# Decode by VectorE alone, expert products shared by each stretch's work, and the stacked visits' causal mask added by VectorE

## The chip, the cores and the metric

The kernel runs on one core of one Trainium2 chip. The time is device time in microseconds from one launch; it is given as the median of several runs. The core has TensorE (PE in the profile, its weight loads PEld), VectorE (DVE), ScalarE (ACT), GpSimd (POOL) and SyncE (SP). Each works off its own queue in the order of the program; DMAs are issued from SP's and ACT's queues. Matmul results land in PSUM, everything else lies in SBUF.

## What is computed

Causal attention with a bias, for 8 batches, 8 heads, 576 positions and 64 columns a head, and behind it a feed-forward layer with a maximum over three products, on 4608 tokens of 512 columns (768 hidden). The three up weights and the down weight come as float64.

```
scores = q @ k.T / 8 ;  cum = cumsum(max(s, 0))
scores = where(key > query, -1e9, scores + min(-(cum_q - cum_k), 0))
attn   = softmax(scores) ;  x = attn @ v
out    = max(max(x @ w1, x @ w2), x @ w3) @ w_out
```

## The kernel before

Products are made from two halves of each operand (a high half and the rest), so that three products stand for one in full precision.

**Visits and steps.** A visit is one batch and one pair of heads (tile names: j is the head of the pair). A step is one visit and one block of 128 queries (qb 0 to 3; qb 4 holds the last 64 queries of both heads). The first 8 visits do qb 0 and 1 of batches 0 and 1 (steps 0 to 15), the next 8 do qb 2 to 4 of the same batches (steps 16 to 39), and 24 further visits do all five (steps 40 to 159). These last ones are called stacked: each head's 64 rows of q and k lie above the 64 rows that carry the bias, so a score block takes two products a head, h and l (`scores`, L379), over the first (qb + 1) x 128 keys. Then PE adds the causal mask as one more product a head, a scaled identity times the 128 x 128 tile `tri`, which holds -1e30 above the diagonal (L385).

**A step** t goes like this (L922 to L952). ACT makes prh, the high half of the probabilities, from the exponentials in PSUM and DVE's reciprocal ri. DVE takes the maximum of the next score block, negated, into nm (`highest`, L450), then what stands in the list `middle`, then prl, the low halves (L505). SP transposes prh and prl by DMA into ph and pl. Evictions that are pending follow, then one group of expert products, then the scores of step t + 2 on PE, the exponentials of step t + 1 on ACT (`expo`, L460, bias nm), then the work that the lists put at this step (`todo`), then more expert groups, and last the value products av of a visit whose probabilities were completed the step before (`values`, L574). Scores have two PSUM buffers, so the scores of step t + 2 wait until prh and prl of step t have been read out.

**Expert groups.** A group is 12 products into one PSUM tile pm (L711), or 18 into po for the output (L753). A set of 256 or 320 tokens has 18 pm groups and 4 po groups. A balance `cost[0]` says whether a step takes groups: each step adds an allowance (4200 ns below step 60, then STEP_NS = 4800) less `pe_cost(t)`, an estimate of PE's other work; each group takes off its own time; groups run while the balance is above zero. What is left over after the last step runs as a tail.

**Decode.** Each of the 24 weight tiles r is 128 x 512 doubles, seen as pairs of 32-bit words lo and hi. ACT makes t from hi (`decode1`, L605), POOL multiplies hi by zero so that only its sign remains (`signs`, L609), DVE joins lo's top bits and the sign (`decode2a`, L613) and then t shifted by three (`decode2b`, L620). After a scale is known, ACT rounds a high half into w (`decode3`, L674), and the low half is made by DVE in one instruction (`decode4`, L684), or for every third tile (the set LOW) by POOL in two (L681, L682). `begun`, `split` and `fetched` give the step of each tile's decode, split and load.

A tile is taken from a pool under a tag; a new tile of the same tag waits until the last reader of the old one is done. The transposed probabilities have the tags pTh and pTl with a number: in the first 16 visits it alternates with the visit, later it is the phase (0 for qb 0 and 1, 1 for the others).

Of the kernel before, what the change touches and what calls it, by code (L numbers as in the profile page):

```python
# [21 lines left out]
def kernel(  # L22
# [9 lines left out]
    nc = tc.nc  # L32
# [22 lines left out]
    STEP_NS = 4800.0  # L55
    NSEC = 0.417
    LOW = set(range(2, 24, 3))
# [133 lines left out]
    zero = const.tile([P, 1], F32, name="zero")  # L191
    nc.gpsimd.memset(zero, 0.0)
# [169 lines left out]
    def scores(t):  # L362
# [7 lines left out]
        if stacked(v):  # L370
# [4 lines left out]
            for x in "hl":  # L375
                for j in range(2):
                    w = r[x, j]
                    if qb < 4:
                        nc.tensor.matmul(  # L379
                            ps[:, j, :nk], lhsT=w[:, qs], rhs=w[:, QP:QP + nk], start=(x == "h"), stop=False,  # L380
                            skip_group_check=True,
                        )
            if qb < 4:
                for j in range(2):
                    nc.tensor.matmul(  # L385
                        ps[:, j, qb * P:nk], lhsT=identb, rhs=tri, start=False, stop=True, skip_group_check=True
                    )
                U[t] = (ps[:, :, :nk], nm, nk)
                return
# [57 lines left out]

    def highest(t):
        sc, nm, _ = U[t]
        nc.vector.tensor_reduce(out=nm, in_=sc, axis=AX.X, op=ALU.max, negate=True)  # L450
# [3 lines left out]
    def expo(t):  # L454
        ps, nm, nk = U[t]
        nj = 2 if nk < S else 1
        sm = small.tile([P, 2], F32, tag="sm", name=f"sm{t}")
        for j in range(nj):
            sc = ps[:, j] if nj == 2 else ps
            nc.scalar.activation(  # L460
                out=sc, in_=sc, func=AF.Exp, bias=nm[:, j:j + 1], accum_out=sm[:, j:j + 1]
            )
        se = small.tile([P, 2], F32, tag="se", name=f"se{t}")
        nc.scalar.activation(out=se[:, :nj], in_=sm[:, :nj], func=AF.Copy, scale=1.0 / PSC, bias=EPS / PSC)
        SE[t] = (se, nj)
# [3 lines left out]
    def probs(t):  # L469
# [5 lines left out]
        if qb in (0, 2):  # L475
            PT[v, ph] = [
                att.tile(
                    [P, 4 + 4 * ph, PH[ph][1]], F16, tag=f"pT{c}{v % 2 if v < NP * NB else ph}", name=f"p{c}{t}", bufs=1
                )
                for c in "hl"  # L480
# [47 lines left out]
    RING = [f"w{n}" for n in (10, 11, 12, 13, 14, 15, 16, 17, 22, 23)]  # L528
# [78 lines left out]
    def signs(i):  # L607
        hi = words(i)[1]
        nc.gpsimd.tensor_tensor(out=hi, in0=hi, in1=zero.to_broadcast([P, N]), op=ALU.mult)  # L609

    def decode2a(i):
        lo, hi = (x.bitcast(I32) for x in words(i))
        nc.vector.scalar_tensor_tensor(  # L613
            out=lo, in0=lo, scalar=29, in1=hi, op0=ALU.logical_shift_right, op1=ALU.bitwise_or
        )

    def decode2b(i):
        lo = words(i)[0].bitcast(I32)
        ti = half.pop(i).bitcast(I32)
        nc.vector.scalar_tensor_tensor(  # L620
            out=lo, in0=ti, scalar=3, in1=lo, op0=ALU.logical_shift_left, op1=ALU.bitwise_or
# [54 lines left out]
    def decode4(i):  # L676
        t = words(i)[0]
        w = pairs_w[i // 2][:, i % 2]
        sw = WS["u" if i < 18 else "d"]
        if i in LOW:  # L680
            nc.gpsimd.tensor_tensor(out=t, in0=t, in1=sw.to_broadcast([P, N]), op=ALU.mult)  # L681
            nc.gpsimd.tensor_tensor(out=w[:, 1], in0=t, in1=w[:, 0], op=ALU.subtract)  # L682
        else:
            nc.vector.scalar_tensor_tensor(  # L684
                out=w[:, 1], in0=t, scalar=sw, in1=w[:, 0], op0=ALU.mult, op1=ALU.subtract
            )
# [100 lines left out]
    def pe_cost(t):  # L787
        v, qb = steps[t]
        nk = min((qb + 1) * P, S)
        c = 4 * nk * NSEC + 200.0  # L790
        if qb == 1:
            c += 1152 * 0.417 + 200.0
        if qb == 4:
            c += 3584 * 0.417 + 200.0
        return c
# [31 lines left out]
    fetched = {5: -1, 7: -1, 8: 0, 9: 0, 10: 1, 11: 1, 12: 2, 13: 2, 14: 3, 15: 3, 16: 4, 17: 4}  # L827
    fetched.update({22: 5, 23: 5, 18: 5, 19: 6, 20: 6, 21: 7})
# [13 lines left out]
    parts2 = {}  # L842
    for i, t in sorted(begun.items(), key=lambda x: (x[1], x[0])):
        parts2.setdefault(t + 1, []).append(i)
    for t, ids in parts2.items():
        (amid if t >= 0 else at)(t, decode2a, ids[0])
        for i in ids[1:]:
            at(t, decode2a, i)
        for i in ids:
            at(t, decode2b, i)  # L850
# [165 lines left out]
```

## Time and profile before

| | |
|---|---|
| median of 3 runs | 944.0 us (943.08 to 945.74) |
| profiled execution | 945.22 us |
| its span, first to last instruction | 943.4 us |
| mean granted TensorE clock | 0.962 |
| instructions | 19,983 |
| largest group, the pm products (L711) | 462.9 us, 3456 products |

Busy shares count an engine's own instructions; PE's matmuls overlap each other, so a product's duration is longer than its share of the time. The idle time of a group is put down to the instruction that released it ("<-"). The lines of the profile on which the prediction rests are shown there.

### The profile page before, as it was taken

What the parts mean: (1) busy time and instruction counts of PE and PEld (TensorE: products, weight loads), DVE (VectorE), ACT (ScalarE), POOL (GpSimd) and SP (SyncE); (2) the same over time, 40 slices, a digit from 0 to 9 for tenths busy, and PEclk for the clock granted to TensorE, in tenths of its full rate; (3) what the DMA queues carried; (4) which work ended last, traced back from release to release, by engine and by line L of the source; (5) the groups of instructions that cost most, each with busy time, mean ns of one, the idle gap of its engine ahead of it and who ended that gap; (6) DMA issues with size and microseconds to landing.
All of it is one profiled execution on the core that took longest, in us unless ns stands there. A gap on an engine that the chain in (4) does not pass through costs nothing. (4 is left out here: it accounts for less than half of the span.)

```text
span 943.4 us, 19983 instructions
## 1 busy us (share of the span) xinstructions
PE 838.6 (89%) x7192; PEld 653.2 (69%) x7192; DVE 582.7 (62%) x1184; ACT 569.4 (60%) x1502; POOL 386.8 (41%) x592
## 2 busy tenths in 40 slices
PE   2456768887779899999999998999999999998998
PEld 2444647765556677877887777877887787776876
DVE  6897885666556575667575666576666656563111
ACT  4667566566467576676676676666667666764111
POOL 4455742222433453635453535454455435430211
PEclk9857999999899999999999999999999999999999
DMA  7974236566577678777778677787676676744000
GB/s 277 237 223 88 58 75 140 115 137 150 118 139 144 119 138 162 152 141 136 157 141 155 134 135 135 135 141 145 133 138 148 127 153 102 139 69 96 2 24 28
DMA packets 242035, 122.34 MB, mean 130 GB/s; under 512 B 217808, under 2 KB 226512, under 8 KB 241936
## 3 DMA queue, kind: packets, MB, share of 16 engines
q1 hardware_dynamic: 237904, 108.74, 58.1%
q10 hardware_dynamic: 4032, 12.32, 4.1%
q8 instruction: 57, 0.93, 0.4%
q14 instruction: 42, 0.34, 0.2%
HBM read 60.18 MB, written 9.44 MB: 74 GB/s over the span
## 5 line engine op out<-in xcount | busy, mean ns | idle before, releaser
L711 PE MATMUL pm<-x,w 128*128 128x256 f16 (+1 forms) x3456 | 462.9, 290 | 3.7 <-ACT m L725 1.7
L711 PEld LDWEIGHTS <-w 128*128 128x128 f16 x3456 | 334.2, 99 | 89.6 <-issue 4.1
L505 DVE SCALAR_TENSOR_TENSOR prl<-s,ri,prh 128x512 f16<-128x512 f32 (+3 forms) x288 | 152.8, 567 | 96.6 <-ACT prh L502 50.4
L717 POOL CAST hh<-m 128x256 f16<-128x256 f32 (+1 forms) x96 | 53.5, 557 | 351.4 <-DVE m L728 294.4
L502 ACT ACTIVATE prh<-s,ri 128x512 f16<-128x512 f32 (+3 forms) x288 | 141.8, 538 | 80.8 <-DVE ri L486 71.7
L450 DVE TENSOR_REDUCE nm<-s 128x1 f32<-128x576 f32 (+4 forms) x160 | 128.0, 800 | 49.3 <-PE s L385 28.9
L460 ACT ACTIVATE s<-s,nm 128x512 f32<-128x512 f32 (+4 forms) x288 | 151.2, 525 | 9.2 <-DVE nm L450 4.1
L753 PE MATMUL po<-hh,w 128*128 128x256 f16 (+1 forms) x768 | 150.4, 287 | 1.5 <-DVE w L684 1.5
L728 DVE SCALAR_TENSOR_TENSOR m<-pm,m 128x256 f32<-128x256 f32 (+1 forms) x192 | 87.1, 454 | 97.4 <-PE pm L711 85.0
L753 PEld LDWEIGHTS <-w 128*128 128x128 f16 x1152 | 110.4, 98 | 31.1 <-DVE w L684 2.1
L753 PE MATMUL po<-hl,w 128*128 128x320 f16 (+1 forms) x384 | 110.0, 287 | 0.9 <-POOL hl L718 0.8
L725 ACT ACTIVATE m<-pm 128x256 f32<-128x256 f32 (+1 forms) x96 | 39.1, 407 | 83.9 <-PE pm L711 80.2
L718 POOL TENSOR_TENSOR hl<-m,hh 128x256 f16<-128x256 f32 (+1 forms) x96 | 74.1, 772 | 7.8
L583 ACT ACTIVATE x<-av 128x256 f16<-128x256 f32 (+1 forms) x64 | 26.3, 410 | 78.6 <-PE av L574 77.9
L138 POOL CAST l<-kb 64x576 fp32r<-64x576 f32 x48 | 32.3, 673 | 100.6 <-PE s L394 75.6
L761 ACT ACTIVATE o<-po,os 128x256 f32<-128x256 f32 (+1 forms) x64 | 31.9, 498 | 65.5 <-PE po L753 50.0
L169 POOL TENSOR_TENSOR l<-raw,h 64x576 fp32r<-64x576 f32 x48 | 68.2, 1422 | 7.2 <-ACT h L155 6.0
L584 DVE SCALAR_TENSOR_TENSOR x<-av,x 128x256 f16<-128x256 f32 (+1 forms) x64 | 29.1, 454 | 59.0 <-ACT x L583 58.9
L574 PEld LDWEIGHTS <-vh 128*64 128x64 f16 x832 | 45.0, 112 | 24.6 <-issue 17.1
L574 PE MATMUL av<-pl,vh 128*64 128x320 f16 (+3 forms) x384 | 56.3, 279 | 5.7 <-DMA pl<-prl 5.6
L379 PE MATMUL s<-h 128*128 128x128 f32 (+1 forms) x192 | 53.7, 361 | 8.4 <-DVE prl L505 7.0
L574 PE MATMUL av<-ph,vh 128*64 128x320 f16 (+3 forms) x384 | 57.5, 287 | 0.6 <-DMA ph<-prh 0.6
(142 smaller groups left out, 1148.2 us busy)
## 6 DMA issues: line engine op xcount, KB each, us to landing
raw<-in_qk_dram SPq DMA_DIRECT2D x96, 304.0 KB, 4.7
r<-in_w_dram ACTq DMA_DIRECT2D x20, 512.0 KB, 4.9
rv<-in_qkv_dram SPq DMA_DIRECT2D x32, 320.0 KB, 3.4
out_dram<-o SPq DMA_DIRECT2D x32, 160.0 KB, 2.0
out_dram<-o SPq DMA_DIRECT2D x32, 128.0 KB, 2.3
raw<-in_qkv_dram SPq DMA_DIRECT2D x8, 480.0 KB, 3.9
ph<-prh SPq DMA_TRANSPOSE x192, 3.3
pl<-prl SPq DMA_TRANSPOSE x192, 2.8
```

Of the source, the lines that this page charges most:

```text
L169: nc.gpsimd.tensor_tensor(out=l[far, QP:V0], in0=raw[far, QP:V0], in1=h[far, QP:V0].bitcast(F32), op=ALU.subtract)
L379: nc.tensor.matmul(ps[:, j, :nk], lhsT=w[:, qs], rhs=w[:, QP:QP + nk], start=(x == "h"), stop=False, skip_group_check=True,)
L450: nc.vector.tensor_reduce(out=nm, in_=sc, axis=AX.X, op=ALU.max, negate=True)
L460: nc.scalar.activation(out=sc, in_=sc, func=AF.Exp, bias=nm[:, j:j + 1], accum_out=sm[:, j:j + 1])
L502: nc.scalar.activation(out=hi, in_=src, func=AF.Copy, scale=sc)
L505: nc.vector.scalar_tensor_tensor(out=lo, in0=src, scalar=sc, in1=hi, op0=ALU.mult, op1=ALU.subtract)
L574: nc.tensor.matmul(av[j * D:(j + 1) * D, c0:nq], lhsT=lt, rhs=rt, start=(n < 2), stop=(n >= len(todo) - 2), skip_group_check=True,)
L711: nc.tensor.matmul(pm[:, :nq], lhsT=w[:, wt, kt, :], rhs=xt, start=(n == 0), stop=(n == 3 * NKT - 1))
L717: nc.gpsimd.tensor_copy(out=st["hh"][:, ft, :nq], in_=m1[:, :nq])
L718: nc.gpsimd.tensor_tensor(out=st["hl"][:, ft, :nq], in0=m1[:, :nq], in1=st["hh"][:, ft, :nq], op=ALU.subtract)
L728: nc.vector.scalar_tensor_tensor(out=m1[:, :nq], in0=pm[:, :nq], scalar=HSC, in1=m1[:, :nq], op0=ALU.mult, op1=ALU.max)
L753: nc.tensor.matmul(pm[:, :nq], lhsT=W[18 + ft][:, wt, dt, :], rhs=st[ht][:, ft, :nq], start=(n == 0), stop=(n == 3 * NFT - 1),)
```

## The change

Five things change.

1. **Decode.** POOL's `signs` goes. DVE shifts t by three in place (`shift`), joins lo's top bits into t (`low_bits`), and joins the sign of hi with t into lo (`sign`): three instructions where it had two. All shifts of a step stand ahead of prl, the rest behind. POOL's part of `decode4` goes to DVE.
2. **Masks of stacked visits.** For qb < 4 the two mask products go. DVE runs one fused instruction a head: it adds a slice of a wide bf16 tile `later` (zeros, then `tri`) to the scores, negates, writes the result over the scores and takes the minimum of it. The exponentials use scale -1. `later` is made by POOL at step 20, in the buffer w23, which leaves the ring of x tiles.
3. **Shares.** `pe_cost` now counts what PE runs in the step itself (the scores of step t + 2, the value products that are due), and the allowances are 4400 and 4700 ns. A helper `leave` is added that nothing calls.
4. **Buffers.** The number in pTh and pTl is the phase for every visit.
5. **Loads** of weights are issued up to two steps earlier.

```
-    STEP_NS = 4800.0
+    STEP_NS = 4700.0
-    LOW = set(range(2, 24, 3))
...
-                            ps[:, j, :nk], lhsT=w[:, qs], rhs=w[:, QP:QP + nk], start=(x == "h"), stop=False,
+                            ps[:, j, :nk], lhsT=w[:, qs], rhs=w[:, QP:QP + nk], start=(x == "h"), stop=(x == "l"),
...
-                for j in range(2):
-                    nc.tensor.matmul(
-                        ps[:, j, qb * P:nk], lhsT=identb, rhs=tri, start=False, stop=True, skip_group_check=True
-                    )
...
+    def later_keys():
+        m = wpool.tile([P, Q4], BF16, tag="w23", name="later")
+        nc.gpsimd.memset(m[:, 0:Q4 - P], 0.0)
+        nc.gpsimd.tensor_copy(out=m[:, Q4 - P:Q4], in_=tri)
+        future.append(m)
     def highest(t):
-        sc, nm, _ = U[t]
+        sc, nm, nk = U[t]
+        if below(t):
+            for j in range(2):
+                nc.vector.tensor_tensor_reduce(
+                    out=sc[:, j], in0=sc[:, j], in1=future[0][:, Q4 - nk:Q4], scale=-1.0, scalar=3.0e38,
+                    op0=ALU.add, op1=ALU.min, accum_out=nm[:, j:j + 1],
+                )
+            return
         nc.vector.tensor_reduce(out=nm, in_=sc, axis=AX.X, op=ALU.max, negate=True)
...
-                    [P, 4 + 4 * ph, PH[ph][1]], F16, tag=f"pT{c}{v % 2 if v < NP * NB else ph}", name=f"p{c}{t}", bufs=1
+                att.tile([P, 4 + 4 * ph, PH[ph][1]], F16, tag=f"pT{c}{ph}", name=f"p{c}{t}", bufs=1) for c in "hl"
...
-    def signs(i):
-        hi = words(i)[1]
-        nc.gpsimd.tensor_tensor(out=hi, in0=hi, in1=zero.to_broadcast([P, N]), op=ALU.mult)
+    def shift(i):
+        ti = half[i].bitcast(I32)
+        nc.vector.tensor_scalar(out=ti, in0=ti, scalar1=3, scalar2=None, op0=ALU.logical_shift_left)
+    def low_bits(i):
+        lo, ti = words(i)[0].bitcast(I32), half[i].bitcast(I32)
+        nc.vector.scalar_tensor_tensor(
+            out=ti, in0=lo, scalar=29, in1=ti, op0=ALU.logical_shift_right, op1=ALU.bitwise_or
+        )
+    def sign(i):
+        lo, hi = (x.bitcast(I32) for x in words(i))
         ti = half.pop(i).bitcast(I32)
         nc.vector.scalar_tensor_tensor(
-            out=lo, in0=ti, scalar=3, in1=lo, op0=ALU.logical_shift_left, op1=ALU.bitwise_or
+            out=lo, in0=hi, scalar=-(2 ** 31), in1=ti, op0=ALU.bitwise_and, op1=ALU.bitwise_or
         )
...
     def pe_cost(t):
-        v, qb = steps[t]
-        nk = min((qb + 1) * P, S)
-        c = 4 * nk * NSEC + 200.0
-        if qb == 1:
-            c += 1152 * 0.417 + 200.0
-        if qb == 4:
-            c += 3584 * 0.417 + 200.0
+        c = 0.0
+        if t + 2 < len(steps):
+            nk = min((steps[t + 2][1] + 1) * P, S)
+            c += max(4 * nk * NSEC * 1.09, 480.0) + (100.0 if nk < S else 150.0)
+        for _, ph in due:
+            c += (3584 if ph else 1152) * 0.417 + 200.0
         return c
...
-        cost[0] = min(cost[0] + (4200.0 if t < 60 else STEP_NS) - pe_cost(t), 4000.0)
+        cost[0] = min(cost[0] + (4400.0 if t < 60 else STEP_NS) - pe_cost(t), 4000.0)
```

What this does to the order of the instructions, at three places. First DVE's queue in the fourth step, where two weight tiles are decoded (r the tile's words, t ACT's product of hi, x and av the value products' eviction). Before:

```order
L486 RECIPROCAL ri_446<-se_393 128x2
L450 TENSOR_REDUCE nm_379<-s_378 128x2
L613 SCALAR_TENSOR_TENSOR r_252<-r_252 128x512
L505 SCALAR_TENSOR_TENSOR prl_449<-s_315,ri_446,prh_448 128x2x128 x2
L584 SCALAR_TENSOR_TENSOR x_0_460<-av_0_433,x_0_460 128x256
L639 TENSOR_REDUCE cnu<-gru_395 128x1
L613 SCALAR_TENSOR_TENSOR r_264<-r_264 128x512
L620 SCALAR_TENSOR_TENSOR r_252<-t_425,r_252 128x512
L620 SCALAR_TENSOR_TENSOR r_264<-t_428,r_264 128x512
L330 SCALAR_TENSOR_TENSOR qkl_492<-st_143,qkh_422 128x256
```

The same place of the same queue after the change:

```order
L496 RECIPROCAL ri_450<-se_394 128x2
L462 TENSOR_REDUCE nm_380<-s_379 128x2
L619 TENSOR_SCALAR t_427<-t_427 128x512
L619 TENSOR_SCALAR t_429<-t_429 128x512
L515 SCALAR_TENSOR_TENSOR prl_453<-s_314,ri_450,prh_452 128x2x128 x2
L594 SCALAR_TENSOR_TENSOR x_0_463<-av_0_437,x_0_463 128x256
L649 TENSOR_REDUCE cnu<-gru_396 128x1
L623 SCALAR_TENSOR_TENSOR t_427<-r_248,t_427 128x512
L623 SCALAR_TENSOR_TENSOR t_429<-r_250,t_429 128x512
L630 SCALAR_TENSOR_TENSOR r_248<-r_248,t_427 128x512
L630 SCALAR_TENSOR_TENSOR r_250<-r_250,t_429 128x512
L331 SCALAR_TENSOR_TENSOR qkl_496<-st_141,qkh_424 128x256
```

Two shifts of t now stand ahead of prl where one instruction on r stood, and four instructions follow behind instead of three; nothing on the way reads what POOL writes.

Second, DVE's queue in a stacked visit, at the maxima of its 384 and 512 wide score blocks (m and pm the expert groups' eviction, h part of the next visit's preparation). Before:

```order
L486 RECIPROCAL ri_3844<-se_3784 128x2
L450 TENSOR_REDUCE nm_3774<-s_3773 128x2
L505 SCALAR_TENSOR_TENSOR prl_3847<-s_3722,ri_3844,prh_3846 128x2x128 x2
L584 SCALAR_TENSOR_TENSOR x_1_3857<-av_1_3815,x_1_3857 128x320
L728 SCALAR_TENSOR_TENSOR m_1_0_3855<-pm_1_0_1_3860,m_1_0_3855 128x320
L160 SCALAR_TENSOR_TENSOR h_1_3795<-raw_1_3679,h_1_3795 64x640
L486 RECIPROCAL ri_3906<-se_3884 128x2
L450 TENSOR_REDUCE nm_3874<-s_3873 128x2
L505 SCALAR_TENSOR_TENSOR prl_3909<-s_3773,ri_3906,prh_3908 128x3x128 x2
```

After the change, from the same block on (ISA names the fused instruction, and with nm alone the read of its accumulator):

```order
L496 RECIPROCAL ri_3863<-se_3814 128x2
L457 ISA s_3805,nm_3806<-s_3805,later 128x384
L457 ISA nm_3806 128x1
L457 ISA s_3805,nm_3806<-s_3805,later 128x384
L457 ISA nm_3806 128x1
L515 SCALAR_TENSOR_TENSOR prl_3866<-s_3745,ri_3863,prh_3865 128x2x128 x2
L594 SCALAR_TENSOR_TENSOR x_1_3875<-av_1_3834,x_1_3875 128x320
L163 SCALAR_TENSOR_TENSOR h_1_3827<-raw_1_3688,h_1_3827 64x640
L496 RECIPROCAL ri_3923<-se_3900 128x2
```

Four instructions stand between ri and prl where one stood, and the eviction of an expert group has moved out of this step, since its groups are dealt out otherwise.

Third, SP's queue at the transposes of the first and second visit, with what each waits for (PE is TensorE, Activation ScalarE, DMAHW a transfer). Before:

```order
L508 DMA_TRANSPOSE ph_254<-prh_258 128x2x128 [waits DMAHW6_49,Activation_49]
L508 DMA_TRANSPOSE pl_255<-prl_259 128x2x128 [waits DMAHW7_49,DVE_49]
L508 DMA_TRANSPOSE ph_254<-prh_303 128x4x128 [waits DMAHW2_49,Activation_49]
L508 DMA_TRANSPOSE pl_255<-prl_304 128x4x128 [waits DMAHW3_49,DVE_49]
L508 DMA_TRANSPOSE ph_362<-prh_366 128x2x128 [waits DMAHW6_49,Activation_49]
```

After the change:

```order
L518 DMA_TRANSPOSE ph_252<-prh_256 128x2x128 [waits DMAHW6_49,Activation_49]
L518 DMA_TRANSPOSE pl_253<-prl_257 128x2x128 [waits DMAHW7_49,DVE_49]
L518 DMA_TRANSPOSE ph_252<-prh_303 128x4x128 [waits DMAHW3_49,Activation_49]
L518 DMA_TRANSPOSE pl_253<-prl_304 128x4x128 [waits DMAHW4_49,DVE_49]
L518 DMA_TRANSPOSE ph_364<-prh_368 128x2x128 [waits DMAHW4_49,DMAHW3_49,DMAHW6_49,PE_49,Activation_49]
```

The second visit's first transpose writes the buffer that the first visit's value products read, so it has gained a wait for PE; the rows behind it on SP stand in order.

More of the change, by code (lines that the diff above doesn't have):

```diff
@@ L113, in load_v, with below @@
         R.setdefault(v, {})["rv"] = t.rearrange("p (j k d) -> p j k d", j=2, d=D)
+    def below(t):
+        v, qb = steps[t]
+        return stacked(v) and qb < 4
     def stacked(v):
@@ L526 @@
     done = set()
-    RING = [f"w{n}" for n in (10, 11, 12, 13, 14, 15, 16, 17, 22, 23)]
+    RING = [f"w{n}" for n in (10, 11, 12, 13, 14, 15, 16, 17, 22)]
     def reserve(tag, b, ph):
@@ L678, in decode4 @@
         w = pairs_w[i // 2][:, i % 2]
[L679 to L686, printed above, removed]
+        nc.vector.scalar_tensor_tensor(
+            out=w[:, 1], in0=t, scalar=WS["u" if i < 18 else "d"], in1=w[:, 0], op0=ALU.mult, op1=ALU.subtract
+        )
         fresh[i] = w.rearrange("p h (a c) -> p h a c", c=P)
@@ L787, in pe_cost, with leave @@
     def pe_cost(t):
-        v, qb = steps[t]
-        nk = min((qb + 1) * P, S)
-        c = 4 * nk * NSEC + 200.0
-        if qb == 1:
-            c += 1152 * 0.417 + 200.0
-        if qb == 4:
-            c += 3584 * 0.417 + 200.0
-        return c
+        c = 0.0
[4 more added lines that the diff above has]
+            c += (3584 if ph else 1152) * 0.417 + 200.0
+        return c
+    due = []
+    def leave(t):
+        v, qb = steps[t]
+        return qb in (2, 3, 4) and stacked(v) and visits[v][1] < NP - 1
     todo = {}
@@ L841 @@
         at(first[v] + 1 if v else -2, vscale2, scale_of(v))
-    parts2 = {}
+    together = {}
     for i, t in sorted(begun.items(), key=lambda x: (x[1], x[0])):
[L844 to L850, printed above, removed]
+        together.setdefault(t + 1, []).append(i)
+    for t, ids in together.items():
+        for f in (shift, low_bits, sign):
+            for i in ids:
+                (amid if f is shift and t >= 0 else at)(t, f, i)
     for i, t in split.items():
@@ L896 @@
         at(t, decode3, i)
-    for i, t in sorted(begun.items()):
+    for i, t in begun.items():
         at(t, decode1, i)
-        at(t, signs, i)
-    for n, (i, t) in enumerate(fetched.items()):
-        (amid if t >= 0 and n % 2 == 0 else at)(t, load_w, i, nc.scalar.dma_start)
+    for i, t in fetched.items():
+        at(t, load_w, i, nc.scalar.dma_start)
     at(1, spread, 1)
+    at(20, later_keys)
     prep2(0)
```

20 lines of the change are left out of this document (5 added, 15 removed).

## The prediction

> **What bounds the kernel now.** I read the page's busy shares and slices first, then the table by stretch, the waits, and last the groups of the stretches that differ.
>
> ```profile
> PE 838.6 (89%) x7192; PEld 653.2 (69%) x7192; DVE 582.7 (62%) x1184; ACT 569.4 (60%) x1502; POOL 386.8 (41%) x592
> ...
> PE   2456768887779899999999998999999999998998
> ...
> DVE  6897885666556575667575666576666656563111
> ...
> 14.00:70.00 56.00, 27.82 (x219) 22.06 (x221) 49.59 (x103) 35.61 (x106) 26.76 (x23) 0.76 0.85 230
> 70.00:142.00 72.00, 48.63 (x409) 37.48 (x409) 60.65 (x114) 46.54 (x116) 41.53 (x43) 0.85 0.34 74
> 142.00:268.00 126.00, 104.78 (x892) 79.58 (x893) 75.30 (x141) 74.89 (x185) 34.00 (x50) 0.94 0.63 134
> ...
> 366.00:864.00 498.00, 488.38 (x4324) 387.00 (x4324) 315.20 (x655) 330.89 (x886) 221.24 (x352) 1.00 0.70 135
> ```
>
> The last four rows are stretches: bounds, length, then busy time of PE, PEld, DVE, ACT and POOL, granted clock, DMA share and GB/s. Two kernels stand here. From 366 to 864 us PE is busy 488 of 498 us at full clock; DVE and ACT are at two thirds. There a microsecond of PE work is a microsecond. From 14 to 142 us, where the weights are decoded, PE is busy 76 of 128 us and DVE 110 of 128, with no other engine near it: there DVE's row of work sets the pace. The middle (142 to 268) has no engine that full, and the change does little in it.
>
> **Masks off PE.** The two mask products per stacked step with qb < 4 go: 24 visits x 4 = 96 steps.
>
> ```profile
> 403.31 0.63 PE L379 MATMUL s<-l 128*128 128x512 f32 x2
> 403.78 0.12 PEld L385 LDWEIGHTS <-identb 128*128 128x128 bf16 x2 [0.28 <-issue]
> 403.78 0.28 PE L385 MATMUL s<-tri,identb 128*128 128x128 bf16 x2
> ...
> 403.90 0.27 PE L753 MATMUL po<-hh,w 128*128 128x256 f16 x1
> ```
>
> A matmul's duration overlaps the next one, so the price is from start to start: the pair starts at 403.78, the next product at 403.90, 0.12 us. 96 x 0.12 = **11.5 us**, nearly all of it where PE is full. Bounds: 0, if PE waits instead, and 96 x 0.28 = 27 us, the pair's undivided time.
>
> **The mask on DVE.** Each of these steps replaces one maximum over both heads by two fused instructions (add the mask, write the scores back to PSUM, take the minimum) and two reads of the accumulator.
>
> ```profile
> L450 DVE TENSOR_REDUCE nm<-s 128x2 f32<-128x1024 f32 x20 | 24.3, 1215 | 12.8 <-PE s L385 12.8
> ...
> L450 DVE TENSOR_REDUCE nm<-s 128x2 f32<-128x256 f32 x32 | 13.0, 406 | 2.3 <-PE s L385 2.2
> ...
> L505 DVE SCALAR_TENSOR_TENSOR prl<-s,ri,prh 128x512 f16<-128x512 f32 x96 | 69.1, 748 | 56.8 <-ACT prh L502 26.7 <-ACT tl L502 20.2 <-DMA pl<-prl 8.8
> ...
> L505 DVE SCALAR_TENSOR_TENSOR prl<-s,ri,prh 128x128 f16<-128x128 f32 x64 | 19.4, 344 | 4.2 <-ACT prh L502 3.3 <-DMA pl<-prl 0.2
> ...
> L486 DVE RECIPROCAL ri<-se 128x2 f32<-128x2 f32 x128 | 20.3, 159 | 20.3 <-ACT se L464 19.0
> ...
> L502 ACT ACTIVATE prh<-s,ri 128x512 f16<-128x512 f32 x96 | 62.0, 680 | 32.2 <-DVE ri L486 28.5 <-DMA ph<-prh 3.5
> ```
>
> No row shows the fused instruction, nor a DVE write to PSUM. The nearest is prl: one operand from PSUM, one from SBUF, a write; (748 - 344) / 384 = 1.05 ns an element over a fixed 210 ns. The nearest of a one-column read is 159 ns. A 512-wide step then takes 2 x 748 + 2 x 159 = 1.81 us for 1.22; a 128-wide one 2 x 344 + 2 x 159 = 1.01 for 0.41. So about 0.6 us more of DVE a step, 96 x 0.6 = 58 us. Low end: the extra instructions' fixed parts vanish in the overlap of neighbours and nothing is added. High end: the write to PSUM doubles the time per element, 1280 x 2 elements a visit x 1.05 ns = 2.7 us on top, 24 x 2.7 = 65 us more. At the chosen value DVE's load in the full stretch rises from 63% to some 75%, so it is no bound. Behind the fused pair on DVE stand prl and the evictions of the expert products; for prl's PSUM buffer the scores after next wait. But prl needs ACT's two prh (0.68 us each at 512), which begin together with the maximum, and these cover most of the delay. I take **+2 us**, between 0 and 15.
>
> The Trainium skill (VectorE: DVE Perf Modes, Rules for kernel authors) speaks against this edit: it advises to minimize the number of DVE operations, since each pays its own flush, and four now stand for one. By its cost row for PSUM sources (the TRN2 errata section, 120 cycles and one per element at 0.96 GHz) a 512-wide fused instruction is an estimated 0.66 us, and DVE's part of the sum would be smaller than mine; no run here shows it yet.
>
> **Decode by DVE alone.** POOL loses 24 sign products and 16 instructions of the low halves; DVE gains 24 shifts and 8 low halves.
>
> ```profile
> L613 DVE SCALAR_TENSOR_TENSOR r<-r 128x512 int32<-128x512 int32 x24 | 23.8, 994 | 11.4 <-POOL r L609 11.4
> L620 DVE SCALAR_TENSOR_TENSOR r<-t,r 128x512 int32<-128x512 int32 x24 | 16.9, 734 | 0.1
> L684 DVE SCALAR_TENSOR_TENSOR w<-r,swu,w 128x512 f16<-128x512 f32 x12 | 13.1, 1132 | 0.0
> ...
> L684 DVE SCALAR_TENSOR_TENSOR w<-r,swd,w 128x512 f16<-128x512 f32 x4 | 5.6, 1442 | 0.0
> ...
> 20.52 0.68 DVE L613 SCALAR_TENSOR_TENSOR r<-r 128x512 int32<-128x512 int32 x1
> ...
> 24.44 1.52 DVE L613 SCALAR_TENSOR_TENSOR r<-r 128x512 int32<-128x512 int32 x1 [0.54 <-POOL r L609]
> ...
> 78.09 1.41 DVE L684 SCALAR_TENSOR_TENSOR w<-r,swu,w 128x512 f16<-128x512 f32 x2
> ...
> 91.80 2.61 DVE L684 SCALAR_TENSOR_TENSOR w<-r,swu,w 128x512 f16<-128x512 f32 x2
> ...
> 92.37 1.49 POOL L681 TENSOR_TENSOR r<-r,swu 128x512 f32<-128x512 f32 x1
> ...
> 5.54 0.44 DVE L234 TENSOR_SCALAR r_t<-s_t 64x576 f32<-64x576 f32 x1
> ```
>
> The same DVE instruction takes 0.68 us alone and 1.52 beside a POOL one; a low half 0.70 at 78.09, and 1.30 at 91.80 beside POOL's at 92.37. So the removal frees DVE of the waits for POOL (11.4), of 24 x (0.994 - 0.68) = 7.5, 24 x (0.734 - 0.68) = 1.3, 12 x (1.132 - 0.70) = 5.2 and 4 x (1.442 - 0.70) = 3.0: 28.4 us. Added are 8 x 0.70 = 5.6 and 24 shifts. A shift, with one operand in SBUF, is nearest to L234, 0.44 us at 576 elements, and I take 0.41; as slow as L613 alone it is 0.68. That is 9.8 (16.3) us. Net: DVE's row loses 28.4 - 15.4 = 13 us (6 or 7 at the high price).
>
> The path gains less, for two waits come next. The first is ACT's t, for which all shifts of a step wait ahead of prl:
>
> ```profile
> 74.37 1.51 DVE L613 SCALAR_TENSOR_TENSOR r<-r 128x512 int32<-128x512 int32 x1 [3.36 <-POOL r L609]
> ...
> 73.30 1.04 POOL L609 TENSOR_TENSOR r<-r,zero 128x512 f32<-128x512 f32 x1 [2.56 <-ACT t L605]
> ```
>
> Of DVE's longest wait for POOL, 3.36 us, only the sign's 1.04 goes; the 2.3 before it were for t, behind three w on ACT. The second: the first stretch's transposed probabilities have one buffer where they had two, and the first transposes of a visit wait for the value products of the visit before.
>
> ```profile
> 31.68 1.17 SPq L508 DMA_TRANSPOSE ph<-prh  x1
> ...
> 37.02 0.22 PE L574 MATMUL av<-ph,vl 128*64 128x128 f16 x2
> ...
> 41.74 0.61 ACT L502 ACTIVATE prh<-s,ri 128x128 f16<-128x128 f32 x2
> ...
> ph<-prh SPq DMA_TRANSPOSE x9, 4.6
> ```
>
> The transposes that started at 31.68 would start after the products that end at 37.2, and SP's queue stands behind them. With 4.6 us to land (median of 20 to 70 us) their source is free at 41.8, as prh of two steps later wants it (41.74). The slack is nil, so each of 7 visits may lose what the decode gained there; I put both waits at 3 us together. The path gains **10 us**, between 0 and 17.
>
> **Products shared anew.** The step allowance and the estimate of PE's other work change. In PE's order, of the steps 60 to 159, 15 held a single expert group or none and no value product, now 2; 15 held three or more groups together with the long value product, now none. The tail after the last step has 47 groups for 44, which costs nothing by itself, since the total is fixed. What can go are PE's waits in the thin steps:
>
> ```profile
> PE s L394 <- DVE prl L505: 4.5, 3, 2.2
> PE s L379 <- DVE prl L505: 3.6, 8, 0.9
> ...
> PEld s L379 <- ACT s L460: 12.1, 16, 3.7
> ```
>
> The first two (268 to 864 us) are 8 us of PE itself; weight loads waited 12.1 more, partly ahead of their turn. I take **-6 us**, between +5 (the even steps wait a little everywhere) and -12. The earlier weight loads, the ring with one slot less and the small mask tile on POOL I cost at nothing: POOL is busy 41%, and the loads only move up in ACT's queue.
>
> **Sum.** -11.5 + 2 - 10 - 6 = -25.5 us. The profiled execution took 945.2 us (span 943.4 and 1.8 around it), 1.2 above the median of the runs, 944.0; against the median that is **918.5 us**.
>
> **Rivals.**
> 1. Freed PE time turns into waits: the longer maximum delays prl and with it the scores after next. For it: prl already ends PE's waits above. Against it: DVE idles a third of the time. The masks then give 0 instead of 11.5, and the maximum costs 5: 933.
> 2. The early gain is eaten: ACT's t or the single buffer sets the pace in POOL's place: 918.5 + 10 = 928.5. For it: the nil slack above. Against it: the low halves' part comes after 70 us, when the DMA share has fallen from 0.85 to 0.34 and transposes should land sooner.
> 3. More than forecast: the early stretch gains 17 and the even steps 12: 905.5. The granted clock of 0.76 up to 70 us would rise as PE idles less, and the score products after prl get shorter. The Trainium skill (TensorE: Matmul & The Clock Gate, Part 1) puts half clock to idle windows of about 3.4 us; the 0.76 agrees with gaps of that kind.
> 4. Slower: the fused instruction takes several cycles an element and DVE becomes the bound of the stacked steps. A visit takes 498 / 20 = 24.9 us (20 maxima of 1024 in that stretch) with 315.2 / 20 = 15.8 of DVE, 3.2 of them in the four maxima (by the two rows above). PE needs 24.4 without the masks, so DVE decides when the eight fused instructions and reads take 11.8; less 8 x (0.21 + 0.16) that is 8.8 us for 2560 elements, 3.4 ns each instead of 1.05. At 4.2 ns, four times the row, a visit is 26.3 us: 24 x 1.4 = +34, less 16 from decode and sharing: 962.
>
> That the change does not do what it says is excluded for the masks: their products are gone from PE's order.
>
> **How the numbers follow.** Forecast 0.54 (907 to 930); rival 1 0.14; rival 2 0.13; rival 3 0.12; rival 4 0.07. The range 902 to 938 leaves out rival 4 and the ends of rivals 1 and 3. A measurement of this kernel tells 0.3% from no change, 941 to 947; rival 1 with its maximum at the high price reaches into that. Faster 0.87, same 0.06, slower 0.07.
>
> **What would show it.** Right: DVE in the stacked steps near 75% and PE still at 98%; fused instructions near 0.75 us at 512; the two decode instructions of the new form at 0.68 us with no wait for POOL; PE's waits for prl shorter; and the first 576-wide maximum, now at 133 us, near 123:
>
> ```profile
> 132.96 0.74 DVE L450 TENSOR_REDUCE nm<-s 128x1 f32<-128x576 f32 x1
> ```
>
> Wrong: PE idles more after 300 us, fused rows far over 1 us, or an early stretch as long as before with DVE idle.

## The result and the profile after

The changed kernel takes **918.27 us** (median of 4 runs, 914.14 to 921.02) where the kernel before took 943.54 (4 runs, 940.88 to 945.74): ratio **0.9716**, 95% interval 0.9663 to 0.9769, that is 27 us less (22 to 32). The forecast was 918.5. The profiled execution of the changed kernel is the fastest of its four, 914.14 us, span 912.3 us; differences between the two profiles are therefore some 6 us larger than those between the medians (31.1 us between the profiled executions, 25.3 between the medians).

The page, busy shares and the slices of PE and DVE:

```profile
PE 823.0 (90%) x7000; PEld 645.5 (71%) x7000; DVE 598.3 (66%) x1504; ACT 568.6 (62%) x1502; POOL 345.7 (38%) x553
...
PE   3557769998799989999999999999999999999998
...
DVE  6898886666467766667676767676677657663111
```

The table by stretch, with the same columns as before (bounds, length, PE, PEld, DVE, ACT, POOL, clock, DMA share, GB/s):

```profile
14.00:70.00 56.00, 29.15 (x229) 23.07 (x229) 50.30 (x127) 38.24 (x110) 7.78 (x6) 0.76 0.78 228
70.00:142.00 72.00, 53.72 (x443) 42.15 (x444) 61.32 (x128) 49.81 (x126) 18.29 (x24) 0.83 0.36 83
142.00:268.00 126.00, 110.91 (x965) 85.72 (x965) 80.04 (x165) 76.75 (x195) 39.83 (x59) 0.96 0.68 144
...
366.00:864.00 498.00, 488.95 (x4263) 388.69 (x4262) 325.46 (x873) 324.32 (x871) 224.10 (x354) 1.00 0.70 131
```

In the first two rows POOL has fallen from 68 to 26 us, and PE gets 83 us of work done there instead of 76, with DVE as full as it was (112 of 128 us). The last row reaches into the tail now; PE is busy 98% of it, as before. DVE from 366 us to the last step, at 830, is busy 318.4 of 464 us, 69%, where it was 63%; 75% was forecast. PE's waits for prl fell from 5.7 us between 366 and 864 us to 1.9 between 366 and 830.

The groups of DVE that are new (line, engine, operation, names, shapes, count, busy us and mean ns, idle time ahead and what ended it):

```profile
L457 DVE CUSTOM_DVE_ANT_0 s<-s,later 128x512 f32<-128x512 f32 x48 | 33.3, 694 | 9.9 <-PE s L380 9.1
L457 DVE DVE_READ_ACCUMULATOR2_ANT nm<- 128x1 f32 x192 | 27.0, 141 | 0.0
...
L630 DVE SCALAR_TENSOR_TENSOR r<-r,t 128x512 int32<-128x512 int32 x24 | 16.6, 724 | 0.2
L623 DVE SCALAR_TENSOR_TENSOR t<-r,t 128x512 int32<-128x512 int32 x24 | 16.0, 698 | 0.0
L689 DVE SCALAR_TENSOR_TENSOR w<-r,swu,w 128x512 f16<-128x512 f32 x18 | 14.1, 836 | 0.0
L457 DVE CUSTOM_DVE_ANT_0 s<-s,later 128x128 f32<-128x128 f32 x48 | 13.9, 289 | 4.3 <-PE s L380 3.4
L619 DVE TENSOR_SCALAR t<-t 128x512 int32<-128x512 int32 x24 | 9.4, 423 | 2.7 <-ACT t L615 2.7
```

The fused instruction takes (694 - 289) / 384 = 1.05 ns an element over 154 ns, and its accumulator's read 141 ns: a 512-wide step 1.67 us for 1.22, 0.45 us more instead of the 0.6 forecast. No instruction of the decode waits for POOL any more; the 2.7 us for ACT's t are what the decode still waits. DVE's timeline at the place of the wait that the forecast named, and at the first 576-wide maximum (start, duration, idle before):

```profile
70.65 0.43 DVE L619 TENSOR_SCALAR t<-t 128x512 int32<-128x512 int32 x1 [2.25 <-ACT t L615]
...
127.83 0.73 DVE L462 TENSOR_REDUCE nm<-s 128x1 f32<-128x576 f32 x1
```

The maximum stood at 132.96 us. It is 5.1 us earlier, not 10: the experiments find part of the rest.

### The profile page after: what moved, and what is told of

Read it like the earlier page. It is cut to its first block, busy times and chain, and to the rows that moved or that the text cites. A ratio compares the mean times of both kernels' runs of the same rounds, so it can differ in the third digit from the quotient of the medians.

```text
span 912.3 us, 19899 instructions
## 1 busy us (share of the span) xinstructions
PE 823.0 (90%) x7000; PEld 645.5 (71%) x7000; DVE 598.3 (66%) x1504; ACT 568.6 (62%) x1502; POOL 345.7 (38%) x553
## 4 chain that ended last, share of the span: by engine, by line
PE 69%; DMA 5%; DVE 4%; ACT 3%; issue 2%; POOL 2%; SPq 1%; ACTq 0%; DVEq 0%; POOLq 0%
PE pm L716 38%; PE po L758 13%; PE av L584 7%; PE s L380 6%; DMA ph<-prh 2%; PE s L391 2%; DMA pl<-prl 2%; DVE prl L515 2%; ACT prh L512 2%; PE s L416 1%; DVE m L733 1%; SPq L524 1%; POOL hh L722 1%; ACT s L472 1%; POOL hl L723 1%
## 5 line engine op out<-in xcount | busy, mean ns | idle before, releaser
L716 PE MATMUL pm<-x,w 128*128 128x256 f16 (+1 forms) x3456 | 455.9, 289 | 4.3 <-DVE m L733 2.2
L722 POOL CAST hh<-m 128x256 f16<-128x256 f32 (+1 forms) x96 | 55.4, 578 | 368.8 <-DVE m L733 310.3
L457 DVE CUSTOM_DVE_ANT_0 s<-s,later 128x128 f32<-128x128 f32 (+1 forms) x192 | 94.7, 493 | 33.4 <-PE s L380 30.0
L584 PE MATMUL av<-pl,vh 128*64 128x320 f16 (+3 forms) x384 | 59.6, 281 | 8.1 <-DMA pl<-prl 8.0
L462 DVE TENSOR_REDUCE nm<-s 128x1 f32<-128x576 f32 (+3 forms) x64 | 49.9, 780 | 22.1 <-PE s L396 12.3
L584 PEld LDWEIGHTS <-vh 128*64 128x64 f16 x832 | 47.8, 112 | 22.4 <-issue 11.1
L472 ACT ACTIVATION_READ_ACCUMULATOR s<-s,nm 128x1 f32 x288 | 57.3, 199 | 0.0
```

The source lines that it names most:

```text
L457: nc.vector.tensor_tensor_reduce(out=sc[:, j], in0=sc[:, j], in1=future[0][:, Q4 - nk:Q4], scale=-1.0, scalar=3.0e38, op0=ALU.add, op1=ALU ...
L472: nc.scalar.activation(out=sc, in_=sc, func=AF.Exp, bias=nm[:, j:j + 1], scale=-1.0 if below(t) else 1.0, accum_out=sm[:, j:j + 1],)
L584: nc.tensor.matmul(av[j * D:(j + 1) * D, c0:nq], lhsT=lt, rhs=rt, start=(n < 2), stop=(n >= len(todo) - 2), skip_group_check=True,)
L716: nc.tensor.matmul(pm[:, :nq], lhsT=w[:, wt, kt, :], rhs=xt, start=(n == 0), stop=(n == 3 * NKT - 1))
L722: nc.gpsimd.tensor_copy(out=st["hh"][:, ft, :nq], in_=m1[:, :nq])
```

## The experiments

Each was timed beside the kernel before; the effect is (ratio - 1) x 943 us, with its 95% interval. A difference between the changed kernel and a variant of it has an interval of 5 to 6 us either way. Item 5 of the change, the earlier loads, was not run alone: the variants of the changed kernel hold it, e1, e2 and e3 do not.

| run | median us | ratio | effect us |
|---|---|---|---|
| the change | 918.27 | 0.9716 | -26.8 (-31.8 to -21.8) |
| e1 masks alone | 934.62 | 0.9901 | -9.3 (-11.8 to -7.0) |
| e2 decode alone | 933.57 | 0.9891 | -10.3 (-12.9 to -7.6) |
| e3 shares alone | 931.93 | 0.9876 | -11.7 (-14.1 to -9.2) |
| e4 change, two buffers | 916.88 | 0.9711 | -27.3 (-30.2 to -24.3) |
| e5 before, masks twice | 948.39 | 1.0062 | +5.8 (+3.3 to +8.5) |
| e6 change, idle POOL products | 928.98 | 0.9841 | -15.0 (-17.5 to -12.4) |
| e7 change, one more maximum | 938.87 | 0.9952 | -4.5 (-6.4 to -2.6) |
| e8 change, masks back on PE | 925.50 | 0.9800 | -18.9 (-21.7 to -16.0) |
| e9 before, no masks | 934.92 | 0.9935 | -6.1 (-8.5 to -3.8) |
| e10 change, old shares | 930.27 | 0.9861 | -13.1 (-14.8 to -11.4) |
| e11 before, groups to the tail | 947.33 | 1.0061 | +5.7 (+3.9 to +7.6) |
| e12 change, more groups early | 927.10 | 0.9836 | -15.5 (-16.9 to -14.0) |

Where in the program the parts act shows in the profiled executions: the start of DVE's reciprocal `ri` of a step, before, and the difference to it in the other kernels (us; the last row is the span). These are single executions, and that of before is 1.7 us above its median. e10 also holds items 4 and 5.

| step | before | change | e1 masks | e2 decode | e3 shares | e10 masks + decode |
|---|---|---|---|---|---|---|
| 17 | 132.9 | -5.1 | +0.6 | -9.8 | +1.4 | -6.8 |
| 40 | 269.2 | -11.5 | +1.2 | -10.3 | -0.7 | -8.7 |
| 60 | 366.0 | -12.9 | -2.3 | -10.9 | +1.1 | -6.6 |
| 159 | 863.7 | -33.3 | -7.3 | -11.1 | -12.5 | -12.2 |
| end | 943.4 | -31.1 | -9.7 | -13.0 | -10.6 | -14.9 |

### e1, e9, e5, e8: what a mask costs on either engine

e1 is item 2 of the change alone, with the tile `later` and the ring without w23:

```
-                for j in range(2):
-                    nc.tensor.matmul(ps[:, j, qb * P:nk], lhsT=identb, rhs=tri, ...)
...
+                nc.vector.tensor_tensor_reduce(out=sc[:, j], in0=sc[:, j], in1=future[0][:, Q4 - nk:Q4], ...)
```

> The kernel before with the mask part alone: the 192 mask products leave TensorE, VectorE adds the mask as it seeks the maximum (the ring of expert buffers is one shorter, as in the change). My sum (masks 11.5 us off TensorE, 2 us back on VectorE) expects 934 us where before has 944, a ratio of 0.990. Rival, freed TensorE time turns into waits for VectorE: 944 us or more, ratio 1.00. If the masks carried all of the gain beyond the decode's, 926 us, ratio 0.982.

e9 takes only the minus lines of it, e5 puts `for again in range(2):` around the two products, e8 undoes item 2 in the changed kernel (the ring stays without w23).

> The kernel before with the masks of the stacked blocks with qb < 4 left out altogether (the output leaves the reference: those blocks see later keys); VectorE's maximum is the one instruction it was. This prices TensorE's side alone. The forecast's term is 11.5 us, 932 us, ratio 0.988, and VectorE's side is then the difference to the masks part, some 2 us. If the price is what doubling the products added, 6 us, 937 us, ratio 0.994, and VectorE's side is a gain of 3. If the longer VectorE work of the masks costs as the added maximum did (20.6 us for 96), removal must be worth 20 us, 923 us, ratio 0.979.

> The kernel before with each of the 192 mask products made twice on TensorE (the output leaves the reference: the masked scores get the mask twice). The forecast's price of 0.12 us for a step's two masks expects 11.5 us more, 955 us, ratio 1.012. If a mask product hides beside other work, 944 to 948 us; if a product costs a full start of its own, up to 27 us more, 971 us.

> The changed kernel with the masks back on TensorE and the maximum as before; decode and shares stay. The forecast's terms (11.5 off, 2 back) expect 9.5 us more than the changed kernel: 928 us, ratio to before 0.983. Rival, the masks' move gains nothing: 918 us, ratio 0.973.

e1 came out at its forecast, -9.3 us, and e8 agrees from the other side (7 us between the medians, 925.5 and 918.3, within its interval). The two halves of the term did not: without any mask the kernel is 6.1 us faster, and with every product doubled 5.8 us slower, where 11.5 was forecast. The price from start to start is not the reason. PE's timeline of e5:

```profile
405.08 0.40 PE L386 MATMUL s<-tri,identb 128*128 128x128 bf16 x4
405.31 0.27 PE L754 MATMUL po<-hh,w 128*128 128x256 f16 x1
```

The four products take 0.23 us from start to start, so the two added ones 0.11, and 96 x 0.11 = 10.6 us. About half of this added PE work never reached the end. Part of it went into PE's idle time: from step 40 to the end of the profiled execution PE idles 17.3 us where it was 21.8.

That e9 is the mirror of this is not shown. The stretch from step 40 to the end, before and in e9 (columns as in the table by stretch):

```profile
269.20:943.40 674.20, 652.38 (x5654) 510.72 (x5653) 388.58 (x808) 407.38 (x1086) 277.05 (x445) 0.99 0.64 122
276.20:939.80 663.60, 641.56 (x5464) 499.02 (x5463) 386.95 (x808) 406.36 (x1085) 276.60 (x445) 1.00 0.65 125
```

PE is busy 10.8 us less and idles as long as before, and the stretch is 10.6 us shorter: here the whole price arrived. This execution lost its time ahead of step 6, where its program is that of the kernel before and ACT was held up at a load:

```profile
52.23 0.42 ACT L319 ACTIVATE qkh<-raw 128x256 fp32r<-128x256 f32 x1 [9.24 <-DMA rv<-in_qkv_dram]
```

Step 6 began 7.4 us late by it. The execution is the slowest of e9's six (941.5 us, median 934.9) and counts in its 6.1 us; between the medians e9 gains 7.7. So doubled PE work arrived by half, and for removed work the record leaves everything between half and all open.

VectorE's side of e1 depends on that. By the ratios e1 is 3 us better than e9, with an interval of about 3.5 either way; in the profiled executions e1 takes 663.3 us from step 40 to the end where e9 takes 663.6. That is not the +2 forecast, but not shown to be a gain either. Its size stays open; that it is small is shown.

### e7: how much room VectorE has

One instruction more ahead of the fused pair:

```
+            idle = small.tile([P, 2], F32, tag="idle", name=f"idle{t}")
+            nc.vector.tensor_reduce(out=idle, in_=sc, axis=AX.X, op=ALU.max, negate=True)
```

> The changed kernel with one more maximum on VectorE in each of the 96 stacked steps, which nobody reads: 0.3 to 1.2 us more of VectorE a step. If VectorE has room there, as the forecast has it, 918 to 922 us, ratio to before 0.975. If VectorE is the bound of these steps, as the first rival has it, half of the added 60 to 70 us or more: 950 us.

It cost 20.6 us between the medians, 0.21 us a step for an instruction of 0.81 us (the mean of its four widths, 1.21, 0.95, 0.68 and 0.40). So neither theory's number: the first rival's mechanism is there, at a quarter of the price. The waits from 366 us to the last step show it, in the changed kernel first:

```profile
ACT s L472 <- DVE nm L457: 4.3, 9, 1.0
...
PE s L391 <- DVE prl L515: 1.1, 1, 1.1
```

and with the added maximum:

```profile
ACT s L474 <- DVE nm L459: 31.6, 39, 2.0
...
PE s L391 <- DVE prl L517: 13.3, 13, 2.3
```

(Waiting engine and line, releaser, us in total, times, longest.) ACT's exponentials come to wait for the maximum, prl slips behind them, and PE's last score block of a visit waits for prl's buffer. At 69% VectorE is not full, but what stands ahead of nm is on a chain. The Trainium skill's rule to minimize VectorE's operations (VectorE: DVE Perf Modes, Rules for kernel authors) agrees with this run; in e1 the instructions that the rule speaks against still came with a gain.

### e2, e6, e4: the decode

e2 is item 1 alone. e6 puts POOL's 24 sign products back where nobody waits for them, behind the decode of the same tile; e4 gives the changed kernel the alternating tags of item 4 back.

```
e6
+    def idle_signs(i):
+        hi = words(i)[1]
+        nc.gpsimd.tensor_tensor(out=hi, in0=hi, in1=zero.to_broadcast([P, N]), op=ALU.mult)
-        for f in (shift, low_bits, sign):
+        for f in (shift, low_bits, sign, idle_signs):
e4
-    ... tag=f"pT{c}{ph}" ...
+    ... tag=f"pT{c}{v % 2 if v < NP * NB else ph}" ...
```

> The kernel before with the decode part alone: no GpSimd products, VectorE makes all shifts, low bits and signs. The forecast's term is 10 us off the path by the first 576-wide maximum, 934 us, ratio 0.989. What the profile after shows there is about 7 us, and another 5 to 8 us between 142 and 268 us that I put to the shares: if these are the decode's too, 929 us, ratio 0.984. Rival, the new wait for ACT's t eats it: 940 us or more.

> The changed kernel with GpSimd's 24 sign products put back, now behind the decode, on words that nobody reads afterwards. If the decode's gain is that VectorE no longer shares the stretch with GpSimd's products, most of it goes: 5 to 8 us more, 924 us, ratio to before 0.979. If it is that VectorE waits no longer, the same as the changed kernel, 918 us, ratio 0.973.

> The changed kernel with two alternating buffers for the transposed probabilities of the pairs, as before. If the single buffer's wait (0.75 us shown at 41.7 us) costs what the forecast put on it, 1 to 3 us less than the changed kernel: 915 to 917 us beside 918, ratio to before 0.970. If it costs nothing, the same as the changed kernel, ratio 0.973.

e2 gives 10.3 us, and its maximum stands where the forecast put it:

```profile
123.17 0.74 DVE L447 TENSOR_REDUCE nm<-s 128x1 f32<-128x576 f32 x1
```

The gain is complete at step 17 and stays to the end. In the changed kernel only half of it is there at step 17, and another 6.4 us come between steps 17 and 40 (-5.1 to -11.5). From the profile after I had put 5 to 8 us of that stretch to the shares, and e10 bears this out: without the shares 1.9 us come there. Why the changed kernel is 4.7 us behind e2 at step 17 is not settled: the shares alone are 1.4 us behind there, a second buffer (e4) brings 0.8, and the earlier loads were not run apart.

In the whole time e4 is 1.4 us below the changed kernel, inside the range expected of a single buffer that costs 1 to 3 us, but far inside the interval of that difference too: it does not decide.

e6 loses 10.7 us between the medians, about all that the decode had gained, though nothing waits for these products. Groups of DVE and POOL in e6:

```profile
L695 DVE SCALAR_TENSOR_TENSOR w<-r,swu,w 128x512 f16<-128x512 f32 x18 | 18.9, 1100 | 0.0
...
L517 DVE SCALAR_TENSOR_TENSOR prl<-s,ri,prh 128x256 f16<-128x256 f32 x16 | 7.0, 475 | 0.9 <-ACT prh L514 0.8
...
L621 DVE TENSOR_SCALAR t<-t 128x512 int32<-128x512 int32 x24 | 14.0, 612 | 2.7 <-ACT t L617 2.7
...
L638 POOL TENSOR_TENSOR r<-r,zero 128x512 f32<-128x512 f32 x24 | 32.1, 1353 | 44.3 <-DVE r L632 31.9 <-PE s L422 6.5 <-ACT m L736 3.9
```

The shift goes from 423 to 612 ns and the low half of w from 836 to 1100, together 24 x 0.189 + 18 x 0.264 = 9.3 us of the 10.7. It depends on what runs beside POOL: 11 of the 24 shifts overlapped a POOL instruction and took 0.59 to 1.26 us, each ending 0.28 us after a POOL instruction did; the other 13 took 0.41 to 0.43. The row of prl tests nothing here, since none of its 16 overlapped one. The kernel before does test it. There prl, whose scores lie in PSUM, ran beside POOL's sign products (the first row is two instructions, 0.47 us each):

```profile
60.42 0.86 DVE L505 SCALAR_TENSOR_TENSOR prl<-s,ri,prh 128x256 f16<-128x256 f32 x2
...
58.72 2.67 POOL L609 TENSOR_TENSOR r<-r,zero 128x512 f32<-128x512 f32 x2
```

Ten of the 16 of this width in the decode's stretch ran beside a POOL instruction and took 468 to 472 ns, the other six 475 to 486.

So what the decode gains can be lost by sharing the stretch with POOL, without any wait for its products. (POOL's next own work came late behind them once: a weight load of PE waited 1.9 us for it.) The test doesn't part the old 11.4 us of waits from the old slow instructions, since the products now stand beside others.

The Trainium skill (SBUF — State Buffer, section SBUF: two separate sides) states that VectorE and GpSimd share a port pair as an exclusive lock, taken by a VectorE instruction with two SBUF inputs (against a GpSimd instruction that reads SBUF) or in a two-port mode. These rows agree: POOL's product reads SBUF, w's low half reads two SBUF tensors, and prl, with one of its inputs in PSUM, is not held up. The shift reads one tensor and writes SBUF; whether it runs in a two-port mode no run shows.

### e3, e10, e11: the shares

e3 is item 3 alone, e10 undoes it in the changed kernel, e11 lowers nothing but the allowance:

```
-    STEP_NS = 4800.0
+    STEP_NS = 4740.0
```

> The kernel before with the shares part alone: expert products placed by the new cost of a step. The forecast's term is 6 us, 938 us, ratio 0.994, of which my reading of the profile after puts 4 us or more between 142 and 268 us. Rival, the shares gain only where the masks have left room on TensorE: 944 us, ratio 1.00, or up to 5 us above it.

> The changed kernel with the shares of before; masks, decode and the other edits stay. If the three parts add up, 12 us more than the changed kernel: 930 us, ratio to before 0.985. If they overlap, as the sum of the three single runs (31 us) against 25 to 27 us suggests, 6 to 7 us more: 924 us, ratio 0.979. If the shares give nothing here, ratio 0.972.

> The kernel before with nothing but a smaller allowance from step 60 on (4740 for 4800 ns), so that 7.2 us of expert groups move from the steps to the tail, as many as the shares move; the estimate of TensorE's other work stays. If these groups fill the tail's wait for the last transposes, about 5 us less, 938.5 us, ratio 0.995. If moving them is worth nothing by itself, as the forecast had it, 943.5 us, ratio 1.00. If it carries the whole of the shares, 932 us, ratio 0.988.

The shares are worth 11.7 us alone and 12.0 in the change (930.27 - 918.27): twice the forecast, at the end of its bounds. What goes from the trace first of all is a pile of DVE's waits from 366 us to the last step. Before:

```profile
DVE x L584 <- ACT x L583: 37.5, 28, 3.1
```

the shares alone (e3):

```profile
DVE x L584 <- ACT x L583: 15.2, 17, 1.7
```

the changed kernel, and the change with the old shares (e10):

```profile
DVE x L594 <- ACT x L593: 14.6, 13, 2.9
```

```profile
DVE x L594 <- ACT x L593: 38.7, 29, 3.1
```

In steps that held three groups together with the long value product, that product ended late; ACT's eviction x waited for it (48.7 us in this stretch before, 28.6 in e3), DVE's x for ACT's, and all of DVE's queue stood behind, prl included. Groups dealt by what PE really runs take this pile away, in e3 and in the change alike, and undoing them brings it back.

But this is not where the time went, as the products in each stretch show. (What follows is an estimate from single executions, with each moved product at its price from start to start in before, 0.114 us at 256 columns and 0.137 at 320.) Between steps 60 and 140 e3 has 67 expert products less, 7.6 us of PE work, and the stretch is 7.7 us shorter; the changed kernel against e10 gives 7.7 and 7.9. So the waits of DVE that went there (29.6 us before, 11.5 in e3) brought next to nothing beyond the work that moved away. The gain stands in two other places. Between steps 17 and 40 e3 does 20 products more (3.0 us) in 2.1 us less, and the changed kernel 21 more in 4.5 less than e10: PE, which idled 23.7 us there before, idles 19.1 in e3. From step 140 to the end e3 does 30 more (3.4 us) in 4.1 us less, the changed kernel in 2.0 less. (Between steps 40 and 60 the two comparisons differ in sign: e3 takes 1.8 us more, the changed kernel 3.5 less.)

The second of these places is the end. The last value products waited for their transposes, before:

```profile
871.03 0.29 PE L574 MATMUL av<-pl,vh 128*64 128x320 f16 x1 [1.07 <-DMA pl<-prl]
872.55 0.30 PE L574 MATMUL av<-pl,vh 128*64 128x320 f16 x1 [1.22 <-DMA pl<-prl]
```

and after the change they don't:

```profile
835.86 2.78 PE L716 MATMUL pm<-x,w 128*128 128x256 f16 x24
838.58 0.33 PE L584 MATMUL av<-ph,vh 128*64 128x320 f16 x2
838.74 0.66 PE L584 MATMUL av<-pl,vh 128*64 128x320 f16 x2
```

From the last score product to the last value product PE took 13.8 us with 60 expert products between in before, and 12.7 with 78 in the changed kernel (12.4 in e3). At 24 products in 2.78 us, 0.116 us each, the 18 more are 2.1 us of work: 3.2 us of waiting went. (In e10 it took 11.7 us with 60, so this wait can also go otherwise, and is no clean part of the shares' gain.)

From this I formed a theory, that groups moved to the tail fill that wait, and e11 took it down. It puts about as many products behind the last scores as the shares do (52 more than before, the shares 54), and is 5.7 us *slower*; its last value products still wait:

```profile
863.19 0.30 PE L574 MATMUL av<-ph,vh 128*64 128x320 f16 x1 [1.14 <-DMA ph<-prh]
864.40 0.30 PE L574 MATMUL av<-ph,vh 128*64 128x320 f16 x1 [0.91 <-DMA ph<-prh]
865.67 0.43 PE L574 MATMUL av<-pl,vh 128*64 128x320 f16 x1 [0.98 <-DMA pl<-prl]
867.04 0.43 PE L574 MATMUL av<-pl,vh 128*64 128x320 f16 x1 [0.94 <-DMA pl<-prl]
```

Fewer groups in the steps are no gain. What e3 has beyond e11 is a choice of which steps get them. It does 37 more products ahead of step 60, where e11 has none more. And the old estimate charges the last two steps for scores and value products that PE doesn't run in them, and so leaves them thin; the new one charges nothing there and puts the groups ahead of the last value products. The new estimate and the allowance of 4400 ns below step 60 were not run apart.

### e12: more groups ahead of step 40

```
-    ... (4400.0 if t < 60 else STEP_NS) ...
+    ... ((4400.0 if t < 16 else 5000.0) if t < 60 else STEP_NS) ...
```

> The changed kernel with an allowance of 5000 for 4400 ns from step 16 to 59, which puts 12.8 us more of expert groups ahead of step 40, where TensorE still waits about 30 us, and takes them from steps 40 to 59. If they fill those waits, about 6 us less than the changed kernel: 912 us, ratio to before 0.967. If the steps only grow by the groups and the later ones cannot shrink below VectorE's and ACT's work, up to 6 us more: 924 us, ratio 0.979.

It was an attempt at a faster kernel, and lost 8.8 us between the medians. The stretches of steps 20 to 39 and 40 to 59 in e12 (columns as in the table by stretch):

```profile
145.00:266.00 121.00, 110.33 (x961) 84.40 (x960) 73.69 (x143) 71.42 (x178) 40.76 (x58) 0.97 0.70 143
266.00:362.00 96.00, 80.14 (x616) 60.91 (x613) 65.10 (x171) 64.39 (x173) 37.96 (x59) 0.89 0.74 142
```

and in the changed kernel:

```profile
143.00:258.00 115.00, 100.14 (x878) 77.69 (x877) 72.71 (x142) 69.62 (x175) 34.28 (x50) 0.96 0.69 148
258.00:353.00 95.00, 88.58 (x710) 66.41 (x708) 64.92 (x173) 65.94 (x177) 41.83 (x68) 0.96 0.77 147
```

The first stretch takes 10 us more of PE work in 6 us more: some of its waits were filled, as hoped. The second does 8 us less and is no shorter. Its groups run out (only two batches are done by then), PE idles, and the clock falls from 0.96 to 0.89. The Trainium skill (TensorE: Matmul & The Clock Gate, Part 1) puts a falling clock to idle windows of TensorE; this row agrees. So steps 40 to 59 have a floor that isn't PE's work.

No run is shown to beat the changed kernel; e4 cannot be told from it.

## Why the prediction came out, point by point

The forecast of 918.5 us held, and so did its reading of the two kernels in one, an early stretch paced by DVE and a late one by PE. But the terms did not all hold. The three parts alone add up to 31.3 us, 5.7 more than the 25.5 forecast, and the changed kernel gains 26.8, 4.5 less than that sum; each of the two differences has an interval about as large as itself. That they nearly cancel is luck.

- **Masks, -11.5 + 2 = -9.5.** The net is right (-9.3); its halves are not shown. The step "there a microsecond of PE work is a microsecond" failed for added work: on a PE 98% busy about half of 10.6 us did not reach the end (e5). For removed work the record is divided, 10.6 us in the one traced execution from step 40 on and 6.1 in the times; by these figures VectorE's side lies between no cost and a gain of 3. The longer maximum cost less than its added 0.45 us for a 512-wide step suggests. The fused instruction at 512 took 0.694 us; I took 0.748 from prl's row. By the cost row of the Trainium skill (VectorE: DVE Perf Modes, TRN2 errata) it was an estimated 0.66 us, a little low.
- **Decode, -10.** Right alone (-10.3; the maximum at 123.17 for "near 123"). The new instructions at 698 and 724 ns and the shift at 423 are near the 680 and 410 taken; w's low half took 836 instead of 700 (744 in the 15 of 18 without a POOL instruction beside them). The wait for ACT's t came as read, 2.25 us at 70.65. Whether the single buffer's share of the 3 us came, e4 is too coarse to say. In the change the gain stands only half complete at the first 576-wide maximum: the forecast's marker failed there. Whether the term holds in the change too is open, since no run takes the decode out of it.
- **Shares, -6.** Mis-sized: -12. The step that failed is the place: I summed PE's waits for prl (8 us) between 268 and 864 us and let the change do little in the middle. The gain came between steps 17 and 40, which the changed kernel passes in 129.9 us (136.3 before, 134.4 with the old shares), and from step 140 to the end. The steps between 60 and 140 gave nothing beyond the work that moved, though 22 us of DVE's waits for ACT's x went from 366 us on. "Costs nothing by itself" for the longer tail does not hold either: e11, which does nothing but lengthen it, is 5.7 us slower.
- **The sum.** Masks and decode together give 13.1 us (e10; 11.4 to 14.8), where alone they give 9.3 and 10.3, 19.6 in sum. 6.5 us of the two are lost beside each other, with an interval of about 4 either way, unless items 4 and 5, which e10 holds beside them, cost some of it. In the profiled executions the loss lies between steps 40 and 60 (table above: -8.7 to -6.6, where the single runs add up to -9.1 and -13.2). e12 found a floor in the same steps, so a gain of PE time there may have nowhere to go; no run tested that. I added terms whose covers are not independent.
- **Rival 1** (PE time turns into waits) holds in part: added PE work went by half into waits, and e7 shows its chain. **Rival 2** (the early gain is eaten) falls at its price of 10 us: e2 has ACT's t and the whole gain, and a second buffer (e4) brings 0.8 us by step 17. **Rival 3** had the 12 us of the shares right as a number and the early stretch's 17 wrong; the granted clock up to 70 us stayed at 0.76. **Rival 4** (a slow fused instruction) falls: 1.05 ns an element where 3.4 would have decided.

## What to carry to other kernels

Price work by removing it *and* by doubling it, and look in the trace at which stretch the difference lies: a pair of products that takes 0.11 us from start to start cost half of that when it was doubled on an engine 98% busy, and between half and all when it was removed. An engine off the critical path can be made to cost by what it shares: GpSimd products that nobody waited for took back about all of the decode's gain, through VectorE instructions that read SBUF alone. When filler work is dealt out by a balance, the estimate of what each step already holds matters more than the amount dealt: about as many products moved to the tail went with -12 us under a better estimate and +6 under a smaller allowance. And waits that vanish need not be the gain: 18 us of DVE's went between steps 60 and 140, whose length followed the moved work alone.

## What was not expected of the hardware

VectorE instructions with an operand in PSUM kept their time beside POOL: in the kernel before prl at 256 took 468 to 472 ns beside a POOL instruction and 475 to 486 without, and in the changed kernel the 15 of the 48 fused instructions at 512 that ran beside one took 0.689 us, the other 33 0.696. A one-input int32 shift in SBUF took 0.41 to 0.43 us alone and 0.59 to 1.26 beside POOL, ending with POOL's instruction (e6). A fused add and minimum that reads and writes PSUM costs 1.05 ns an element, no more than prl's multiply into SBUF.
